# Four blocks of six chunks: a 20-product scheme over whole experts in a Mamba-2 and expert-merge kernel

## The chip, the cores and the metric

One core of a Trainium2 chip runs the whole kernel. The time is the device time of one execution in microseconds; it is taken several times, and the median is quoted. One execution was also taken by the hardware profiler, and all views below come from that one. PE is the matrix engine, PEld its weight loads, DVE the vector engine, ACT the scalar engine, POOL the general engine, and SP the engine whose queue issues nearly all transfers.

## What is computed

There are two stages. The first is a chunked state-space scan (4 sequences, 8 heads, 768 positions, head width 32, state width 16). The second merges four experts over the same 3072 tokens of width 256, with the tokens' heads laid side by side.

```python
# stage 1, per chunk: la = log(clip(a)); cum = cumsum(la)
M = (C @ B.T) * exp(cum_i - cum_j) * causal
y = M @ x + (C @ state) * exp(cum_i)
state = exp(sum la) * state + sum_j exp(cum_last - cum_j) * B_j x_j
# stage 2, x = y laid out as (3072, 256); E = 4, F = 1024
p = probs / (probs.sum(-1, keepdims=True) + 1e-9)
for e in range(E):
    out += p[:, e:e+1] * (maximum(x @ w1[e], 0) @ w2[e])
```

All of it is float32.

## The kernel before

The kernel works with 24 chunks of 128 positions. Two chunks make a *pair* of 256 tokens. The 16 *slices* of the hidden dimension are 256 wide, four to an expert. A *block product* is one 256-wide slice half against 256 tokens: `product()` issues it as two matmul calls (two 128-row halves of the contraction) into one bank of PSUM, and the profile shows four matmul records for it. Every matmul of the experts is issued there, so line L913 carries all of them.

Plain block multiplication of a slice with a pair takes two products a layer for each output half. The kernel saves products by bilinear schemes in the manner of Strassen: sums of weight blocks times sums of token blocks, and combinations of the results.

- Scheme `B` covers two slices x two halves x two pairs in 7 products for 8.
- Scheme `H` covers three slices x two halves x three pairs in 15 products for 18.

`ORDER` cuts the tokens into five blocks: three of four chunks (`B`) and two of six (`H`). Within a block a *unit* is one expert under `B` (two pairs of slices) or three slices under `H`; 16 slices do not divide by three, so that each `H` block has a sixth unit with one plain slice. For each unit and layer:

- `operands()` loads the weights, forms the sums of weight blocks (`scheme.sums`, line L1004) on DVE or POOL, and stores them in DRAM (`w_d`); later blocks load the stored sums. The sums for `H` are formed early, on POOL, at the units in `EARLY`.
- `token_sums()` forms the sums of token blocks, once a block (L1023).
- `twos_first()` and `threes_first()` issue the first layer's products. Results are kept with copies by ACT (`snap`, L922), put back into a bank to go on accumulating (`seed`, L927), corrected on DVE (`combine`, L940; a subtraction in the bank, L1050 or L1089), and then gated: `gated` (L948) does the ReLU and the multiplication by the expert's probability in one DVE instruction.
- `twos_right()` and `threes_right()` form the second layer's inputs from the gated blocks (`combine`, L940).
- `second()` issues the second layer by *houses*, pairs of accumulators that share a bank. `visit()` seeds the bank from the accumulator's copy, adds the products, and copies it back by ACT (L1190).
- `result()` combines a block's accumulators into its output (L1242); `leave()` transposes on DVE (L1287) and stores. The last block leaves by `leave_last()`, with transposes on PE (L1311).

The second layer of a unit is merged with the first layer of the next: `put()` spreads the two lists evenly in PE's order. PE's order is thus written out in `line`. Scans for the next block are put into it at positions in `PAIRS_AT`: `scores()` for the matmuls of C and B (L487), `outputs()` for the chunk's outputs and state (L531, L859). The decay matrix of chunks 0 to 3 is made by scans on DVE (L504); that of the later chunks by exponentials on ACT (L511) with a causal cut on POOL (L516), from cumulative sums that went through DRAM (`cum_d`).

The orders of the other engines come from `Plan.run()`, which places each step at build time by expected durations and due times, chooses between DVE and POOL where both can do it, and hands out buffers: 33 of kind V (gated blocks, copies, accumulators), 28 of kind W (weights), 8 banks. The engines' queues are fixed by that; at run time they only wait for each other.

Of the kernel before, what the change touches and what calls it, by code (L numbers as in the profile page):

```python
# [22 lines left out]
NV, NW = 33, 28  # L23
SLACK, BACK, YIELD = 0.0, 3.0, 0.0
EARLY = 2, 3, 4, 5, 6, 7, 8, 9, 10, 11
SOFT = 1
ROUND = 0, 3, 2, 0, 4
# [8 lines left out]
SCORED = 4  # L36
BUSY, CALM = 200.0, 1.06
AHEAD = 3
SOON = 3
BARE = 2  # L40
EASY = 40.0
HELD = ("x", "w"), (5, 8), (0, 7)
APART = (0, 7),
TAILS = 4, 4, 2, 0, 0, 0
LAST = (0, 1), (0, 2), (1, 1), (1, 2), (0, 0), (1, 0)
LATE = (13, 2), (6, 9), (11, 4), (10, 12), (3,), (1, 14), ("x", "w"), (5, 8), (0, 7)

PAIRS_AT = {
    (0, 2): ((1, 9, "s0"), (2, 1, "s1"), (2, 18, "o01")),
    (4, 2): ((0, 1, "s0"), (2, 1, "s1"), (2, 14, "o01")),  # L50
    (4, 3): ((0, 1, "s0"), (1, 1, "o0"), (1, 1, "s1"), (2, 1, "s2"), (2, 14, "o12")),
    (6, 3): ((0, 1, "s0"), (0, 14, "o0"), (2, 1, "s1"), (3, 1, "s2"), (3, 14, "o12")),
}
# [27 lines left out]
class Plan:  # L81
# [12 lines left out]
    def add(self, on, fn, reads=(), writes=(), part=(), lag=None, due=None, reuse=None, two=False,  # L94
            port=True, after=None, kb=0, hold=0.0, pieces=1, behind=()):
        w = Work(on, fn, (.16 if "PE" in on else .09) if lag is None else lag)
        w.hold = hold
        w.two, w.port, w.after, w.kb, w.pieces = two, port, after, kb, pieces
# [49 lines left out]
    def homed(self, w, at):  # L148

        taken, when = {}, at  # L150
        for v in w.touched:
# [7 lines left out]
            if v.seeded:  # L159
                spare = [h for h in spare if h.full]  # L160
            elif v.kind == "bank":
                hollow = [h for h in spare if not h.full and h.free <= at]
                spare = hollow or spare
# [24 lines left out]
    def run(self, line, at, begin):  # L188
# [19 lines left out]
        while todo:  # L208
# [4 lines left out]
            for w in waiting[e]:  # L213
# [5 lines left out]
                if len(w.on) > 1 and e == "POOL":  # L219
                    if max(ready, now) + w.on[e] > w.latest + late + SLACK or self.backlog(  # L220
                            waiting["DVE"], now, t["DVE"], w) < (BACK if now > EASY else 99):
                        continue
# [81 lines left out]
class Scheme:  # L304
# [4 lines left out]
H = Scheme()  # L309
H.rows, H.pairs = 3, 3  # L310
H.blocks = dict.fromkeys(
    (1, 2), {3: (0, 0), 9: (0, 1), "b": (1, 0), 13: (1, 1), 7: (2, 0), 0: (2, 1)})
H.sums = ((12, "b", 13, 1), (2, "b", 7, 1), (11, 12, 7, 1), (5, 11, 0, 1), (10, 3, 12, 1),
          (8, 10, 9, 1), (1, 8, 0, 1), (6, 1, 7, 1), (14, 5, 9, 1), (4, 3, "b", 1))
H.tokens = (("e", (0, 2), (0, 0), -1), (11, "e", (1, 2), -1), ("g", (1, 2), (1, 0), -1),
            (2, (1, 2), (0, 2), -1), (13, "g", "e", -1), (6, (0, 0), (0, 1), 1),
            (3, 6, (0, 2), -1), (10, "e", (1, 1), -1), (14, (1, 2), 6, -1),
            (4, (1, 1), (0, 1), -1), (1, 6, (1, 1), -1), (9, (1, 1), "g", -1))
H.right = {0: (1, 0), 5: (1, 2), 7: (0, 0), 8: (1, 1), 12: "e"}
H.shared = {1: ((12, 11), (6, 5), (2, 10), (14, 8), (4, 1)),  # L320
            2: ((2, 11), (4, 1), (14, 6), (5, 8), (10, 12))}
H.houses = ((13, 2), (11, 4), (0, 7), (1, 14), (6, 9), (5, 8), (10, 12), (3,), ("x", "w"))
H.plain = {(0, 0): 7, (1, 0): 0, (1, 1): 8, (1, 2): 5, (0, 1): "x", (0, 2): "w"}
# [7 lines left out]
B.right = {1: (0, 0), 2: (1, 0), 3: (1, 1)}  # L331
B.shared = {1: ((6, 7), (5, 3)), 2: ((7, 5), (6, 3))}
B.houses = ((1, 2), (3, 7), (5, 6), (4,))
ORDER = B, B, B, H, H
# [9 lines left out]
def kernel(  # L344
# [24 lines left out]
    NG = 5  # L369
# [4 lines left out]
    for scheme in ORDER:  # L374
        blocks.append(Block(scheme, sum(b.n for b in blocks)))
    assert NSEQ == 4 and E * EPB == 3 * NG + 1 and sum(b.n for b in blocks) == NCH

# [28 lines left out]
    def some(n, shape, name, pool=const):  # L406
# [15 lines left out]
        "gate": some(3, [P, max(b.n for b in blocks), P], "gate"),  # L422
# [23 lines left out]
    def load_decays(c, ab):  # L446
        src = acut_d if c < NSEQ else cum_d
        nc.sync.dma_start(
            out=ab, in_=src[real(c)].rearrange("h s -> (h s)").partition_broadcast(P))
# [120 lines left out]
    for fb in range(0, 4, 2):  # L570
        load_w1(fb, homes["W"][fb])
# [47 lines left out]
    for fb in range(4, 8, 2):  # L619
        load_w1(fb, homes["W"][fb])  # L620
    load_tokens(3, xb[3])
    for fb in range(0, 4, 2):
        load_w2(fb, homes["W"][fb + 1])
    load_decays(3, homes["ab"][0])
# [139 lines left out]
    def fetch(c):  # L764
# [9 lines left out]
        if "ab" not in s and c >= SPREAD:  # L774
            s["ab"] = value("ab")
            dma(lambda e: load_decays(c, s["ab"].t), 1, 512, part=[s["ab"]],
                reads=[cd] if c >= NSEQ else [])

    def decays(c):
# [5 lines left out]
        if c < NSEQ:  # L785
            for part in range(2):
# [4 lines left out]
                else:  # L791
                    half = NH * P // 2
                    dve(1.15, lambda e, lo=half * part: scan(
                        LT0[:, j], s["ab"].t[:, lo:lo + half], lo), two=True,
# [29 lines left out]
    def scores(cs):  # L824
# [6 lines left out]
        for r in (3, 2, 0, 1):  # L831
            def fn(e, r=r):
# [3 lines left out]
                nc.vector.tensor_mul(to, g, LT0[:, js, h] if cs[0] < NSEQ else to)  # L836

            dve(D512 if len(cs) > 1 else D256, fn, reads=[gs_[r], *(LTv if cs[0] < NSEQ else ())],
# [6 lines left out]
    def outputs(cs):  # L845
# [23 lines left out]
        for c in cs:  # L869
# [5 lines left out]
                out=yt.t[:, :, lo:lo + P], in_=v(y)[:, :, 0:P]), reads=[y], part=[yt])  # L875
            if c < NCH - NSEQ:
                s["A"] = value("A")
                act((.1, .4, .2, .4)[turn_of(c)], lambda e, c=c, s=s, y=y: keep_state(
                    c, s["A"].t, v(y)[:, :, P:]), reads=[y], part=[s["A"]])
# [89 lines left out]
    def operands(k, scheme, fbs, l, after=None, due=None, loaded={}):  # L969

        load, half = ((load_w1, w1_half), (load_w2, w2_half))[l - 1]
        where = {}
        for f, fb in enumerate(fbs):
            v = loaded.get((fb, l)) or value("W")
            used = {x[1] for r, x in scheme.blocks[l].items() if x[0] == f and r != "b"}
            if (fb, l) in loaded:
                pass
            elif len(used) == 1 and (*fbs, l, 0) in w_d:
                i, = used
                dma(lambda e, v=v, fb=fb, i=i: nc.sync.dma_start(  # L980
                    out=half(v.t, i), in_=source(fb, l, i).rearrange(
                        "p (j f) -> p j f", j=JJ) if l == 1 else source(fb, l, i)),
                    kb=128, part=[v], after=after)
            else:
                dma(lambda e, v=v, fb=fb: load(fb, v.t), part=[v], after=after)
            for r, x in scheme.blocks[l].items():
                if x[0] == f:
                    where[r] = v, x[1]
        shared = [value("W") for _ in scheme.shared[l]]
        for v, pair in zip(shared, scheme.shared[l]):  # L990
            for j, r in enumerate(pair):
                where[r] = v, j

        def view(r):
            v, i = where[r]
            return (half if r in scheme.blocks[l] else w1_half)(v.t, i)

        keys = [(*fbs, l, i) for i in range(len(shared))]
        if keys[0] in w_d:
            for key, v in zip(keys, shared):  # L1000
                dma(lambda e, v=v, key=key: nc.sync.dma_start(out=v.t, in_=w_d[key]), part=[v])
        else:
            for r, x, y, sign in scheme.sums:
                plan.add({"POOL": .72} if due else B256, lambda e, r=r, x=x, y=y, sign=sign: (  # L1004
                    on(e).tensor_add if sign > 0 else on(e).tensor_sub)(view(r), view(x), view(y)),
                    two=True, reads=[where[x][0], where[y][0]], part=[where[r][0]])
            for key, v in zip(keys, shared):
                d = stored_sums(key)
                dma(lambda e, v=v, d=d: nc.sync.dma_start(out=d, in_=v.t), reads=[v],
                    due=due or (lambda v=v: v.readers[-1]))  # L1010
        weights[k, fbs, l] = where, view

    def token_sums(k):
        Y, scheme = {}, blocks[k].scheme

        def get(x):
            return (yT[k, x[1]], lambda v, i=x[0]: v.t[:, i]) if isinstance(x, tuple) else (
# [8 lines left out]
        for r in {r for h in scheme.houses for r in h} - {"x", "w"}:  # L1026
            tokens[k, r] = get(scheme.right.get(r, r))
# [7 lines left out]
    def opener(k, fbs, seq):  # L1035
# [3 lines left out]
        def mul(r, into=None):  # L1039
# [490 lines left out]
```

## Time and profile before

| | us |
|---|---|
| median of 3 runs | 626.41 (626.35 to 628.62) |
| the profiled execution: its own time | 627.55 |
| the profiled execution: span from first to last instruction | 625.8 |
| busy PE, PEld, DVE, ACT, POOL | 616.6, 526.3, 487.0, 328.2, 167.8 |
| L913, the expert products: records | 1572 + 824 + 244 = 2640 |
| granted PE clock | 1.000 |
| bytes moved by DMA | 127.46 MB, 63.7% of 16 engines' time on the main queue |

A line of groups names the source line, the engine, the operation, output <- inputs, shapes and the count; then the busy time, the mean duration in ns of one, and the engine's idle time just before them with what ended it. A line of the chain of waits gives a start, a length and what the time went to. Records of PE overlap, so the time for one product is read from the chain and not from the groups.

### The profile page before, as it was taken

What the parts mean: (1) busy time and instruction counts of PE and PEld (TensorE: products, weight loads), DVE (VectorE), ACT (ScalarE), POOL (GpSimd) and SP (SyncE); (2) the same over time, 40 slices, a digit from 0 to 9 for tenths busy, and PEclk for the clock granted to TensorE, in tenths of its full rate; (3) what the DMA queues carried; (4) which work ended last, traced back from release to release, by engine and by line L of the source; (5) the groups of instructions that cost most, each with busy time, mean ns of one, the idle gap of its engine ahead of it and who ended that gap; (6) DMA issues with size and microseconds to landing.
All of it is one profiled execution on the core that took longest, in us unless ns stands there. A gap on an engine that the chain in (4) does not pass through costs nothing.

```text
span 625.8 us, 10435 instructions
## 1 busy us (share of the span) xinstructions
PE 616.6 (99%) x3429; PEld 526.3 (84%) x3429; DVE 487.0 (78%) x842; ACT 328.2 (52%) x763; POOL 167.8 (27%) x227
## 2 busy tenths in 40 slices
PE   9999989999999999999999999999999999999997
PEld 4788778888888888888888888888888888888886
DVE  6999998865638778475788997959897987869684
ACT  5477558634358644636855635446444335465441
POOL 4015645731135564424754102200000000000010
PEclk9999999999999999999999999999999999999999
DMA  7898879983799776579999828636232424953001
GB/s 235 275 346 272 279 244 316 321 285 98 218 306 305 234 241 210 146 235 339 305 358 317 267 48 260 204 103 193 62 93 67 130 44 111 351 161 114 1 1 50
DMA packets 112629, 127.46 MB, mean 204 GB/s; under 512 B 28980, under 2 KB 78144, under 8 KB 112576
## 3 DMA queue, kind: packets, MB, share of 16 engines
q1 hardware_dynamic: 112420, 126.74, 63.7%
q8 instruction: 27, 0.44, 0.3%
q14 instruction: 26, 0.21, 0.1%
q10 hardware_dynamic: 156, 0.06, 0.0%
HBM read 101.87 MB, written 24.89 MB: 203 GB/s over the span
## 4 chain that ended last, share of the span: by engine, by line
PE 91%; DVE 4%; DMA 2%; ACT 2%; issue 1%; SPq 0%; DVEq 0%; ACTq 0%
PE bank L913 86%; PE bank L487 2%; PE bank L531 2%; DMA ab<-cum_d 1%; DVE w L1004 1%; DVE v L940 1%; DVE v L948 1%; PE bank L669 1%; PE bank L859 1%; DMA w<-in_w_dram 0%; PE bank L645 0%; ACT MT L511 0%; DVE bank L1089 0%; ACT bank L927 0%; DVE MT L836 0%
## 5 line engine op out<-in xcount | busy, mean ns | idle before, releaser
L913 PE MATMUL bank<-v,w 128*128 128x256 f32 x1572 | 376.7, 380 | 3.2 <-DVE v L948 1.7
L913 PEld LDWEIGHTS bank<-v,w 128*128 128x128 f32 x1572 | 296.6, 190 | 49.2 <-issue 2.9
L913 PE MATMUL bank<-Y,w 128*128 128x256 f32 x824 | 210.6, 379 | 0.0
L913 PEld LDWEIGHTS bank<-Y,w 128*128 128x128 f32 x824 | 156.3, 190 | 21.9 <-issue 0.3
L940 DVE TENSOR_TENSOR v<-v,v 128x512 f32<-128x512 f32 x187 | 132.7, 730 | 33.6 <-ACT v L922 32.4
L948 DVE SCALAR_TENSOR_TENSOR v<-bank,gate 128x512 f32<-128x512 f32 x149 | 102.0, 687 | 45.7 <-PE bank L913 36.4
L927 ACT COPY bank<-v 128x512 f32<-128x512 f32 (+1 forms) x177 | 99.6, 571 | 58.1 <-DVE v L940 43.6
L922 ACT COPY v<-bank 128x512 f32<-128x512 f32 x101 | 58.9, 584 | 82.5 <-PE bank L913 80.6
L1004 POOL TENSOR_TENSOR w<-w,w 128x256 f32<-128x256 f32 x93 | 76.4, 840 | 54.8 <-PE bank L913 31.5
L1190 ACT COPY v<-bank 128x512 f32<-128x512 f32 x95 | 55.4, 584 | 65.8 <-PE bank L913 65.4
L913 PE MATMUL bank<-LT,w 128*128 128x256 f32 x244 | 62.6, 380 | 0.0
L511 ACT ACTIVATE MT<-ab,neg 128x128 f32<-128x128 f32 x160 | 51.2, 390 | 6.1 <-DMA ab<-cum_d 3.2
L913 PEld LDWEIGHTS bank<-LT,w 128*128 128x128 f32 x244 | 46.0, 190 | 7.1 <-issue 0.7
L516 POOL TENSOR_SCALAR_AFFINE_SELECT MT<-MT 128x512 f32<-128x512 f32 x40 | 29.8, 747 | 81.3 <-ACT MT L511 76.1
L940 DVE TENSOR_TENSOR v<-bank,v 128x512 f32<-128x512 f32 x37 | 25.4, 688 | 8.9 <-PE bank L913 6.9
L940 POOL TENSOR_TENSOR LT<-LT,v 128x512 f32<-128x512 f32 x1 | 1.6, 1580 | 110.5 <-DVE LT L940 110.5
L940 POOL TENSOR_TENSOR v<-v,v 128x512 f32<-128x512 f32 x4 | 6.2, 1546 | 75.7 <-DVE v L948 73.4
L836 DVE TENSOR_TENSOR MT<-bank,MT 128x512 f32<-128x512 f32 x40 | 24.8, 680 | 1.8 <-PE bank L487 1.6
L948 DVE SCALAR_TENSOR_TENSOR LT<-bank,gate 128x512 f32<-128x512 f32 x23 | 15.8, 686 | 11.3 <-PE bank L913 7.8
L940 DVE TENSOR_TENSOR v<-v,LT 128x512 f32<-128x512 f32 x29 | 22.3, 768 | 0.6 <-PE bank L913 0.2
L1004 DVE TENSOR_TENSOR w<-w,w 128x256 f32<-128x256 f32 x45 | 21.4, 507 | 0.3 <-DMA w<-in_w_dram 0.3
L1089 DVE TENSOR_TENSOR bank<-bank,v 128x512 f32<-128x512 f32 x22 | 15.3, 694 | 6.8 <-PE bank L913 6.7
(115 smaller groups left out, 372.2 us busy)
## 6 DMA issues: line engine op xcount, KB each, us to landing
w<-w_d SPq DMA_DIRECT2D x138, 256.0 KB
w<-in_w_dram SPq DMA_DIRECT2D x126, 256.0 KB
w_d<-w SPq DMA_DIRECT2D x82, 256.0 KB
ab<-cum_d SPq DMA_DIRECT2D x20, 512.0 KB
w<-in_w_dram SPq DMA_DIRECT2D x42, 128.0 KB
gate<-p_d SPq DMA_DIRECT2D x10, 384.0 KB
xb<-in_xbc_dram SPq DMA_DIRECT2D x17, 192.0 KB
gate<-p_d SPq DMA_DIRECT2D x11, 256.0 KB
```

The costliest lines, as they stand in the source:

```text
L487: nc.tensor.matmul(out=views[r][:, j], lhsT=xb[j][k, OBT:OBT + P], rhs=ctm[j][k].rearrange("p t s -> p (t s)"), start=(j == 0), stop=True, ...
L511: nc.scalar.activation(out=MT[:, place(c, h), 0:P], in_=ab[:, h * P:h * P + P], func=AF.Exp, bias=neg[:, h % NT, NQ * real(c) + h // NT:NQ ...
L516: nc.gpsimd.affine_select(out=MT[:, h:h + n, 0:P], in_=MT[:, h:h + n, 0:P], compare_op=ALU.is_ge, fill=0.0, base=0, pattern=[[0, n], [1, P ...
L836: nc.vector.tensor_mul(to, g, LT0[:, js, h] if cs[0] < NSEQ else to)
L913: nc.tensor.matmul(out=o, lhsT=w[:, j], rhs=x if half is None else x[:, j], start=(start and j == 0), stop=(j == 1), skip_group_check=True)
L922: act(.5, lambda e: nc.scalar.copy(out=flat(v), in_=bank.t), reads=[bank], writes=[v])
L927: act(.54 if to - lo > FB else .32, lambda e: nc.scalar.copy(out=bank.t[:, lo:to], in_=flat(v)[:, lo:to]), reads=[v], writes=[bank])
L940: plan.add(engines, lambda e: (on(e).tensor_add if sign > 0 else on(e).tensor_sub)(flat(v), whole(x), whole(y)), reads=[x, y], writes=[v], ...
L948: dve(D512, lambda e: nc.vector.scalar_tensor_tensor(out=h.t, in0=whole(x).rearrange("p (j m) -> p j m", j=JJ), scalar=0.0, in1=g.t[:, 2 * ...
L1004: plan.add({"POOL": .72} if due else B256, lambda e, r=r, x=x, y=y, sign=sign: (on(e).tensor_add if sign > 0 else on(e).tensor_sub)(view(r ...
L1089: dve(D512, lambda e: nc.vector.tensor_sub(b5.t, b5.t, flat(t)), reads=[t], writes=[b5])
L1190: act(.5, lambda e: nc.scalar.copy(out=flat(v), in_=bank.t), reads=[bank], writes=[v])
```

## The change

All tokens go in four blocks of six chunks under a new scheme `G`: four slices x two halves x three pairs, 20 products for 24. A unit is one expert. The schemes `H` and the plain sixth unit are gone. The first unit (expert 0, block 0) is different, because at that time only the first pairs of chunks exist: its first pair goes plain, the second and third by `B`, and `fold()` adds what `B` accumulated into the accumulators of `G`. The order of experts in each block is such that the last expert of a block is the first of the next, whose weights are then still there; so expert 0's sums for `G` are first formed at the end of the second block. `operands()` forms all sums the first time an expert is met (POOL where it can, DVE where a sum is late, by `lean`), stores them, and from then on loads them, with the four unsummed halves that the scheme needs packed in two buffers. `result()` works in the accumulators themselves. Chunks 4 and 5, which now belong to the first block, get their decays by scans on DVE. Buffers of kind V are 35, gates 2 instead of 3.

```diff
-NV, NW = 33, 28
+NV, NW = 35, 28
-EARLY = 2, 3, 4, 5, 6, 7, 8, 9, 10, 11
+LEAN = 4.0
+SCANNED = 6
+SCORED, OWN, LEAD, LEFT, MARK = 5, 3, 5, 3, 5
+FILLED = 3
+ORDERS = (0, 1, 2, 3), (3, 1, 2, 0), (0, 1, 2, 3), (3, 1, 2, 0)
+PAIRS_AT = ((1, 24, "s0"), (2, 1, "o0"), (2, 1, "s1"), (2, 24, "s2"), (3, 1, "o12")), (
+    (1, 1, "s0"), (1, 24, "s1"), (2, 1, "o01"), (2, 24, "s2"), (3, 1, "o2"))
...
             elif v.kind == "bank":
-                hollow = [h for h in spare if not h.full and h.free <= at]
+                hollow = [h for h in spare if not h.full and (
+                    h.free <= at or sum(x.full for x in spare) <= FILLED)]
...
-                if len(w.on) > 1 and e == "POOL":
+                if w.lean:
+                    if e == "DVE" and w.latest + late > max(ready, now) + LEAN:
+                        continue
+                elif len(w.on) > 1 and e == "POOL":
...
+G = Scheme()
+G.pairs = 3
+G.blocks = dict.fromkeys((1, 2), {
+    "a": (0, 0), 16: (0, 1), "c": (1, 0), 10: (1, 1), 13: (2, 0), "d": (2, 1), 11: (3, 0), "e": (3, 1)})
+G.raw = (16, 10), (13, 11)
+G.sums = ((15, 13, 10, -1), (9, 11, 10, -1), (0, "a", 16, -1), (2, "c", 11, -1), (1, "c", 13, -1),
...
+G.houses = (house(7, 9), house(15, 10), house((2, 19), (3, 17)), house(11, 13), house(12, 14),
+            house(4, 8), house((1, 6), (5, 18)), house(0, 16))
...
-ORDER = B, B, B, H, H
+BLOCKS = 4
...
-        if c < NSEQ:
+        if c < SCANNED:
             for part in range(2):
...
+    def fours_first(k, fbs):
...
+        b10 = mul(10)
+        s31 = snap(b10)
+        b13 = mul(13)
+        s23 = snap(b13)
+        adjust(b10, s23, -1)
+        b16 = mul(16)
+        s14 = snap(b16)
+        adjust(b13, s14)
+        b11 = mul(11)
+        s26 = snap(b11)
+        mul(15, b10)
+        s18 = snap(b10)
+        mul(9, b11)
+        b3 = adjust(b11, s31, 1, value("bank", seeded=True))
+        mul(0, b16)
+        gate(0, 0, b16)
+        mul(2, b11, [b3])
+        s20 = snap(b11)
+        gate(1, 2, combine(b11, s31))
+        mul(1, b10)
+        gate(1, 1, b10)
+        adjust(b10, s20)
+        mul(14, b13)
+        s19 = snap(b13)
+        gate(3, 2, mul(3, b3))
+        gate(1, 0, mul(7, b10))
+        gate(2, 1, mul(18, seed(s18)))
+        gate(2, 2, mul(17, b13))
+        adjust(b13, s23, -1)
+        b8 = mul(8, seed(s14))
+        b6 = adjust(b8, s26, -1, value("bank", seeded=True))
+        gate(0, 2, mul(19, seed(s19)))
+        mul(5, b8, [b6])
+        gate(3, 1, combine(b8, s26, -1))
+        gate(0, 1, mul(6, b6))
+        gate(2, 0, mul(12, b13))
+        gate(3, 0, mul(4, b8))
...
+    def fours_right(h):
+        T = {0: h[0, 0], 3: h[3, 2], 4: h[3, 0], 6: h[0, 1], 7: h[1, 0], 12: h[2, 0], 18: h[2, 1],
+             19: h[0, 2]}
...
+        T[11] = combine(T[9], v, -1, reuse=v)
+        T[13] = combine(w, T[15], -1)
...
+        into(9, A[9], A[10])
+        into(14, A[14], A[13])
...
+        if k < len(blocks) - 1:
+            for r, sign, x in parts.values():
+                into(r, A[r], A[x], sign)
+            return [A[r][0] for r in (0, 1, 2)]
...
+    plain = [plain_first(fb) for fb in range(4)]
...
+    own_ = visit(0, house(0, 16), [
+        (((0,), (16,))[d], weights["S", fb, 2], lambda fb=fb, d=d: w2_half(weights["S", fb, 2].t, d),
+         plain[fb][1]) for fb in range(4) for d in range(2)])
+    line.extend(own_[:OWN])
+    outputs([2, 3])
...
+    line.extend(fill[:SCORED - OWN])
+    scores([4, 5])
+    line.extend(fill[SCORED - OWN:len(fill) - LEFT])
+    outputs([4, 5])
...
+    for k in range(BLOCKS):
+        for g in ORDERS[k][not k:]:
+            units.append((k, tuple(range(4 * g, 4 * g + 4))))
```

## Prediction

> **What bounds the kernel now.** I read the page first, then the chain of waits, PE's waits, a table by stages, and the vector groups in two stretches.
>
> ```profile
> span 625.8 us, 10435 instructions
> ...
> PE 616.6 (99%) x3429; PEld 526.3 (84%) x3429; DVE 487.0 (78%) x842; ACT 328.2 (52%) x763; POOL 167.8 (27%) x227
> ...
> PE   9999989999999999999999999999999999999997
> ...
> DVE  6999998865638778475788997959897987869684
> ...
> L913 PE MATMUL bank<-v,w 128*128 128x256 f32 x1572 | 376.7, 380 | 3.2 <-DVE v L948 1.7
> ...
> L913 PE MATMUL bank<-Y,w 128*128 128x256 f32 x824 | 210.6, 379 | 0.0
> ...
> L913 PE MATMUL bank<-LT,w 128*128 128x256 f32 x244 | 62.6, 380 | 0.0
> ```
>
> PE is busy for 99%. The three groups of L913 (the expert products) hold 1572 + 824 + 244 = 2640 matmul records. Reading the loops gives the same work as block products: a block under B is 8 pairs of slices x 7 x 2 layers = 112, three of them 336; a block under H is 5 triples x 15 x 2 plus 12 plain = 162, two of them 324; 660 in all, so four records to a product. What one costs in the queue is read from long pieces of the chain of waits, since single records overlap:
>
> ```profile
> 241.48 0.59 PE bank L859 x16
> 242.07 1.12 PE bank L531 x32
> ...
> 281.13 0.72 PE bank L859 x32
> 281.86 2.10 PE bank L531 x64
> ...
> 335.48 39.91 PE bank L913 x184
> ...
> 417.61 199.63 PE bank L913 x924
> ```
>
> 39.91 / 46 = 0.868 us and 199.63 / 231 = 0.864 us: a product is 0.866 us. The upper lines are the chunk outputs: 1.71 us for a pair of chunks alone, 2.82 us for two pairs together. The rest of the span is small: some 13 us before the first product, about 4 us after the last, and these waits:
>
> ```profile
> PE bank L913 <- DVE v L948: 1.7, 1, 1.7
> PE bank L913 <- ACT bank L927: 1.3, 2, 0.7
> PE bank L487 <- ACT v L1193: 1.1, 1, 1.1
> ```
>
> The table by stages (busy us of PE, PEld, DVE, ACT, POOL in each window) puts them in time:
>
> ```profile
> 13.00:46.00 33.00, 32.60 (x191) 26.43 (x184) 30.07 (x63) 20.91 (x57) 2.33 (x4) 1.00 0.94 314
> 46.00:100.00 54.00, 50.63 (x335) 42.20 (x334) 50.53 (x85) 35.60 (x100) 28.12 (x40) 1.00 0.86 275
> ...
> 335.00:600.00 265.00, 265.00 (x1345) 231.61 (x1338) 217.87 (x364) 129.45 (x258) 17.73 (x15) 1.00 0.46 140
> ```
>
> PE idles 0.4 us up to 46 and 3.4 us from 46 to 100, where DVE is 94% busy; 0.6 us more near 199, then nothing to the tail: 4.4 us in flight. From 335 to 600, all H, DVE at 82% costs PE nothing. So the time is products times 0.866 us plus chunk work, and DVE is the next limit, first of all in the opening.
>
> **The change part by part.** *Products.* The new kernel has 16 (block, expert) units; 15 run scheme G, 20 products for each of two layers, so 600. The first (expert 0, block 0) runs before all three pairs exist: pair 0 plain, 4 slices x 2 x 2 layers = 16; pairs 1 and 2 by B, 2 x 7 x 2 = 28. Together 644, that is 16 fewer, all on PE's queue: 16 x 0.866 = -13.9 us. This is the main term.
>
> *Chunk matmuls.* The same 24 chunks. Grouping of outputs: before, two doubles in B (2 x 2.8), then twice a single and a double (9.0; the last is smaller), about 14.4 us; after, one single (1.7) and three times single plus double (13.3), about 15.0. Price +0.7 us.
>
> *Large vector work (128x512).* An H unit has 10 corrections, 9 gates, 13 second-layer sums: 32 for 30 products, 1.07 each. B has 20 for 28, 0.71. G has 8 corrections, 12 gates, 16 second-layer sums: 36 for 40, 0.90. Totals are 566 before and 564 after. G thus loads DVE less than the H stage, which hides its work completely: 36 x 0.69 = 24.8 us in a unit of 40 x 0.866 + about 1.7 chunk work = 36.3 us. On the path: 0. If that cover went, it would be paid as in the third rival.
>
> *Small vector work (128x256, 0.42 us).* Result sums: 7 per B block and 23 per H block = 67 before; 22 per block and 8 in fold() = 96 after. Token sums 36 before, 52 after. Together 45 x 0.42 = +19 us of DVE over the whole run, 3 points of its share, beside PE. Result sums have a unit to finish in; token sums of a new block read pairs that are put out a unit ahead. 0 on the path; late, each transition could cost the five-sum chain to G's first product, 2.1 us x 3. The in-place results leave 8 accumulators where an H block held 9 and 7 more buffers, so I see no new buffer wait there.
>
> *ACT.* A G unit has 7 snapshots, 3 seeds and up to 16 house copies, 26 x 0.58 = 15 us of 36: hidden. Chunks 4 and 5 move from 16 exponentials (16 x 0.39 = 6.2 us of ACT) and 4 causal cuts on POOL to 4 scans on DVE at the 1.22 us which the row of L504 for chunk 3 shows: +4.9 us of DVE before about 32 us.
>
> *Weights.* Sums: 164 before (104 on POOL at 0.84 us, 60 on DVE at 0.5), spread over two thirds of the run. After: 16 for the first unit and 32 for each expert, 144. Those of experts 1 to 3, 96 of them, fall due between about 46 and 186 us. POOL alone needs 32 x 0.84 = 27 us a unit, and about 5 us of chunk work, in 36 us: it fits with little to spare, and DVE takes what is late. SP's queue carries fewer weight bytes: 8 units reloaded at 40 x 131 KB (42 MB), 4 built at 2.1 MB in and 4.2 MB out (25 MB), 2 MB for the first; 69 MB, against 96 MB in the rows of loads and stores now. A reloaded unit moves 5.2 MB in 36 us, 145 GB/s; the H stage ran at 140 GB/s with no PE wait. A unit holds 20 of the 28 weight buffers, more than H's; loads that wait for a buffer hold up what is behind them on SP (gates, chunk inputs, result stores), but none stands late for PE in the H stage. 0, with the bound in the first rival.
>
> *Opening.* Two stretches pull apart. The own second-layer products put 7 products (6.0 us) between the first scores and their outputs, where 16 records (3.8 us) do it now: a gain of at most the 0.4 us lost there. Against it, expert sums, four more scans and twelve G token sums meet B's work on DVE; and the stored decays must come back for chunk 4 by about 33 us. Its row: the store leaves at 28.9 now and must leave near 20. Bounds on all PE stalls in flight: 0 (everything hidden, as after 200) and about 18 (twice the rate of 46 to 100, 2 x 3.4 / 54, held to 186). I take 6.0 us, nearest to the row of 46 to 100, for a stage of similar density that lasts about twice as long but has fewer stores: +1.6 us against the 4.4.
>
> *Sharing between DVE and POOL.* Two stretches of the same trace, with many POOL sums and with none:
>
> ```profile
> L1004 POOL TENSOR_TENSOR w<-w,w 128x256 f32<-128x256 f32 x19 | 16.7, 897 | 13.7 <-PE bank L913 7.8 <-DMA w_d<-w 5.7
> ...
> L940 DVE TENSOR_TENSOR v<-v,v 128x512 f32<-128x512 f32 x18 | 15.2, 868 | 3.5 <-ACT v L922 3.4
> ```
>
> ```profile
> L940 DVE TENSOR_TENSOR v<-v,v 128x512 f32<-128x512 f32 x18 | 11.8, 682 | 1.7 <-ACT v L922 1.7
> ```
>
> The first is 200 to 250, the second 450 to 500. An add of two buffers grows by 868 - 682 = 186 ns; 16 of them in a unit are 3 us, within the 11.5 us which a G unit leaves free on DVE. That is what I use. The Trainium skill, page "SBUF — State Buffer", section "Who interferes with whom", speaks against this change: the two engines share one port pair as an exclusive lock, held for the whole instruction, the loser fully blocked. If by that rule all 32 sums of a unit each held up DVE for their 0.72 us, it would be 23 us, 11.5 us over the slack, and three such units would make the sum 650 us. The rows agree with a lock that is sometimes met, not each time.
>
> *Tail.* Now: a plain unit's first six products, then 36 alone; after: 20 alone behind the last G first layer. Second-layer inputs of the last products (slice 3) are needed from the fourth house on, 6 products (5.2 us) later. 0, up to 2.
>
> *Sum* against the profiled execution's own 627.55 us (span 625.8): 627.55 - 13.9 + 0.7 + 1.6 = 615.95. The median of the runs shown lies 1.14 below that execution: 614.8, rounded to **615 us**.
>
> **The rivals.** (1) *Weight sums become the bound, slower than before.* While experts are first built, POOL sums slow to 1.18 us (three in 3.54 us at 220 in the timeline): 32 x 1.18 + 5 = 43 us against 36.3, and a first product waits for its weight: 6.5 us for each of experts 1, 2, 3, and perhaps 0: 19.5 to 26 us, giving 633 to 639. It decides from a unit losing 4.4 us (13.2 / 3). For: DVE is 94% busy in the opening and can't help. Against: DVE's own sum takes 0.42 us, and the sums run over 140 us, not just when needed. 0.13.
>
> (2) *The decays of chunks 4 and 5 come late.* One row in the chain, a load of stored decays, took 7.99 us under a saturated DMA. If outputs 4 and 5 wait that long, 3 to 8 us more than my sum: 618 to 623. For: DMA is at 0.94 there. Against: the new opening stores no weight sums ahead of it. 0.17.
>
> (3) *G's chain inside its banks.* One bank goes through six corrections, gates and seeds; each is ACT 0.58 + DVE 0.69, and 3.5 us of other products cover it. If DVE's backlog adds 0.5 to 1 us a unit, 15 units lose 7 to 15: 622 to 630, no measurable change. Against: H has such chains and PE shows no wait for them. 0.07.
>
> (4) *Stalls vanish.* Down to 1 us in flight: 609 to 611. 0.08.
>
> **How the numbers follow.** The forecast, 611 to 618, has the remaining 0.55. The range from 610 to 624 takes in it, the second rival, most of the fourth's upper part and the lower edge of the third: about 0.79. A difference of 0.5% (3.1 us) is about the least that a measurement of this kernel can tell. Faster: 0.55 + 0.17 + 0.08 = 0.80; same: 0.07; slower: 0.13.
>
> **What would show it.** Right: L913 with 2576 records (644 x 4) and 0.866 us a product in the chain; PE idle below 8 us between 13 us and the tail, most of it before 150; DVE near 82%; no recurring PE wait from 190 on. The first rival shows as PE waiting on w of L1004 or its loads at 75 and 114 us, the second as one PE wait at L859 or L531 near 33 us, the third as equal waits in every unit. More than 13 us of new PE idle makes the prediction wrong in sign.

## The result and the profile after

The changed kernel took 623.12 us (median of six executions, 621.46 to 624.35) beside 627.0 us of the kernel before on the same chip (six executions). The ratio is 0.9929, 95% interval 0.9903 to 0.9956: faster by 0.7%, some 4 us, where 11 to 12 us were forecast. The time is inside the range on record; the forecast of 615 us is missed by 8. The profiled execution took 624.35 us, 3.2 less than the profiled one of before.

The page of the changed kernel, the rows that answer to those of before (L924 is now the line of the products):

```profile
span 622.6 us, 10073 instructions
...
PE 606.6 (97%) x3365; PEld 515.1 (83%) x3365; DVE 498.7 (80%) x852; ACT 291.7 (47%) x681; POOL 180.9 (29%) x240
...
PE   9979989989999999999999999999999999999997
...
DVE  6879897998879987497877989487695988576675
...
POOL 6586962973262110696700110110000000000000
PEclk9999989999999999999999999999999999999999
...
L924 PE MATMUL bank<-v,w 128*128 128x256 f32 x1672 | 394.7, 381 | 5.2 <-DVE v L959 2.5
...
L924 PE MATMUL bank<-Y,w 128*128 128x256 f32 x692 | 177.7, 381 | 4.2 <-DVE bank L1062 1.8
...
L924 PE MATMUL bank<-LT,w 128*128 128x256 f32 x212 | 54.0, 380 | 0.0
```

1672 + 692 + 212 = 2576 records: 644 products, as forecast. PE's share fell from 99% to 97%. The digits say where: the slices (15.6 us each) that show a 7 or an 8 among PE's nines lie, but for the last, in the first ten, and one of them has a granted clock below nine. These ten hold more than half of POOL's work. The chain of waits gives the products when nothing is late:

```profile
280.56 69.26 PE bank L924 x320
...
427.16 185.83 PE bank L924 x860
```

69.26 / 80 = 0.866 us to a product, 185.83 / 215 = 0.864. So the unit price held, and what went wrong lies between products. PE's waits inside the span of the products, all before 156 us but that of the tail:

```profile
PE bank L924 <- DVE v L959: 2.5, 3, 1.8
PE bank L924 <- POOL w L1015: 2.0, 1, 2.0
PE bank L924 <- DVE bank L1062: 1.8, 1, 1.8
PE bank L924 <- DVE Y L1034: 1.4, 1, 1.4
PE bank L870 <- ACT v L1208: 0.9, 1, 0.9
...
PE bank L1316 <- DVE LT L1251: 0.7, 1, 0.7
PE bank L924 <- DMA w<-in_w_dram: 0.6, 1, 0.6
PE bank L924 <- ACT v L885: 0.4, 1, 0.4
PE bank L924 <- ACT bank L938: 0.4, 1, 0.4
```

They sum to 10.0 us without the tail's 0.7 (L1316); the forecast allowed 6.0, before had 4.4. One of them is for a weight sum on POOL (L1015, at 78 to 80 us), four are for DVE in the opening (34.7, 43.5, 51.7, 53.0 us), one is for DVE at 140 us. The table by windows right after the wait on POOL (busy us of PE, PEld, DVE, ACT, POOL; granted clock; DMA share; GB/s):

```profile
79.00:80.00 1.00, 0.02 (x1) 0.05 (x1) 1.00 (x3) 0.00 (x0) 1.00 (x3) 1.00 0.75 233
80.00:81.00 1.00, 1.00 (x3) 0.82 (x4) 1.00 (x3) 0.00 (x0) 1.00 (x2) 0.53 0.54 162
81.00:82.00 1.00, 1.00 (x4) 0.81 (x3) 0.63 (x3) 0.00 (x0) 1.00 (x3) 0.50 0.60 198
82.00:83.00 1.00, 1.00 (x3) 0.74 (x3) 0.68 (x1) 0.00 (x0) 1.00 (x3) 0.50 0.01 4
```

The wait is followed by over 3 us at half the clock, in which the first eight records take 3.66 us in place of 1.73: the wait costs 2.05 us and 1.9 behind it. A table by two long windows, the changed kernel first, the kernel before below:

```profile
13.00:155.00 142.00, 131.82 (x834) 107.55 (x828) 125.41 (x206) 76.79 (x215) 92.77 (x118) 0.99 0.66 214
155.00:612.00 457.00, 456.86 (x2422) 396.50 (x2421) 361.02 (x610) 208.35 (x450) 79.12 (x98) 1.00 0.47 145
```

```profile
13.00:155.00 142.00, 138.22 (x788) 116.25 (x781) 120.27 (x217) 85.97 (x222) 55.86 (x77) 1.00 0.84 275
155.00:612.00 457.00, 456.39 (x2513) 395.27 (x2512) 352.17 (x583) 235.14 (x523) 104.19 (x127) 1.00 0.59 186
```

After 155 us PE is as full as it was. Before, it loses 10.2 us where it lost 3.8; POOL works 92.8 us of the 142 where it worked 55.9, DVE is busy for 88% and gets through fewer instructions (206 for 217) in more time.

The balance by the starts of PE's records, after minus before: products 16 x 0.864 = -13.8 us; gaps between products +8.1 (15.0 for 6.9: above all the waits, 5.6 more, and the half clock, 1.9); all else, that is chunk work with its waits, the time ahead of the first product and the tail, +2.5 (51.7 for 49.2). Sum -3.2. The forecast had -13.9, +1.6 and +0.7.

### The profile page after: what moved, and what is told of

The parts are those of the page before. It is cut to its first block, busy times and chain, and to the rows that moved or that the text cites. A ratio compares the mean times of both kernels' runs of the same rounds, so it can differ in the third digit from the quotient of the medians.

```text
span 622.6 us, 10073 instructions
## 1 busy us (share of the span) xinstructions
PE 606.6 (97%) x3365; PEld 515.1 (83%) x3365; DVE 498.7 (80%) x852; ACT 291.7 (47%) x681; POOL 180.9 (29%) x240
## 4 chain that ended last, share of the span: by engine, by line
PE 82%; DVE 8%; DMA 5%; issue 2%; POOL 1%; ACT 1%; SPq 0%; DVEq 0%; POOLq 0%; ACTq 0%
PE bank L924 79%; DVE v L951 2%; DVE v L959 1%; DMA ah<-cum_d 1%; DMA ab<-acut_d 1%; POOL w L1015 1%; DMA w<-in_w_dram 1%; PE bank L498 1%; PE bank L542 1%; DVE Y L1034 1%; DMA acut_d<-v 1%; DVE w L1015 1%; DVE MT L847 1%; DMA ab<-cum_d 1%; PE bank L870 0%
## 5 line engine op out<-in xcount | busy, mean ns | idle before, releaser
L924 PE MATMUL bank<-v,w 128*128 128x256 f32 x1672 | 394.7, 381 | 5.2 <-DVE v L959 2.5
L924 PEld LDWEIGHTS bank<-v,w 128*128 128x128 f32 x1672 | 317.3, 191 | 53.0 <-issue 4.8
L924 PE MATMUL bank<-Y,w 128*128 128x256 f32 x692 | 177.7, 381 | 4.2 <-DVE bank L1062 1.8
L924 PEld LDWEIGHTS bank<-Y,w 128*128 128x128 f32 x692 | 130.0, 190 | 26.1 <-DVE bank L1062 2.4
L1015 POOL TENSOR_TENSOR w<-w,w 128x256 f32<-128x256 f32 x95 | 81.8, 882 | 34.4 <-PE bank L924 21.7
L1062 DVE TENSOR_TENSOR bank<-bank,v 128x512 f32<-128x512 f32 x86 | 58.6, 695 | 34.1 <-PE bank L924 23.2
L938 ACT COPY bank<-v 128x512 f32<-128x512 f32 x129 | 74.5, 591 | 12.3 <-DVE v L959 8.7
L924 PE MATMUL bank<-LT,w 128*128 128x256 f32 x212 | 54.0, 380 | 0.0
L924 PEld LDWEIGHTS bank<-LT,w 128*128 128x128 f32 x212 | 40.1, 190 | 6.0 <-DVE v L959 0.3
L1015 POOL TENSOR_TENSOR w<-w 128x256 f32<-128x256 f32 x32 | 27.0, 853 | 18.0 <-PE bank L924 12.3
L491 ACT ACTIVATE ctm<-xb,tmask 128x128 f32<-128x128 f32 x48 | 15.8, 391 | 10.3 <-DMA xb<-in_xbc_dram 10.0
L1251 DVE TENSOR_TENSOR v<-v,v 128x256 f32<-128x256 f32 x51 | 19.9, 425 | 0.8 <-ACT v L1204 0.5
L959 DVE SCALAR_TENSOR_TENSOR v<-v,gate 128x512 f32<-128x512 f32 x26 | 18.8, 724 | 0.4
```

Source lines behind the costliest of these rows:

```text
L924: nc.tensor.matmul(out=o, lhsT=w[:, j], rhs=x if half is None else x[:, j], start=(start and j == 0), stop=(j == 1), skip_group_check=True)
L938: act(.54 if to - lo > FB else .32, lambda e: nc.scalar.copy(out=bank.t[:, lo:to], in_=flat(v)[:, lo:to]), reads=[v], writes=[bank])
L959: dve(D512, lambda e: nc.vector.scalar_tensor_tensor(out=h.t, in0=whole(x).rearrange("p (j m) -> p j m", j=JJ), scalar=0.0, in1=g.t[:, 2 * ...
L1015: plan.add(B256, lambda e, r=r, x=x, y=y, sign=sign: (on(e).tensor_add if sign > 0 else on(e).tensor_sub)(view(r), view(x), view(y)), two= ...
L1062: dve(D512, lambda e: (nc.vector.tensor_add if sign > 0 else nc.vector.tensor_sub)(to.t, bank.t, whole(x)), reads=[x, bank], writes=[to])
L1251: plan.add(engines, lambda e: (on(e).tensor_add if sign > 0 else on(e).tensor_sub)(o[1](), x[1](), y[1]()), reads=[v for v in vs if v is n ...
```

## The experiments

Three theories of the gaps stood against each other. **A**: the sums of weights, now packed into the first 155 us (144 in all, formed when an expert is first met), load POOL and through it DVE. **B**: the stored decays of chunks 4 and 5 come back late; the load `ab<-acut_d` stands in the chain with 7.41 us from 24.18, and the wait at 34.7 hangs behind it. **C**: it is G's own chain between PE, ACT and DVE, as in the third rival. A was split later: **A1**, POOL has no time for the sums, as in the first rival; **A2**, POOL's reading of buffers slows DVE's sums, so DVE is late. All ratios are against runs of the kernel before on the same chip.

| kernel | median us | ratio, 95% interval |
|---|---|---|
| weight sums 8 columns wide | 616.57 | 0.9835, 0.9811 to 0.9859 |
| chunk 5's decays not loaded | 621.24 | 0.9920, 0.9894 to 0.9945 |
| both | 616.81 | 0.9841, 0.9816 to 0.9866 |
| POOL dearer in the plan | 621.66 | 0.9912, 0.9881 to 0.9944 |
| POOL fills, reads hardly | 616.65 | 0.9830, 0.9792 to 0.9869 |
| all weight sums on DVE | 628.90 | 1.0037, 1.0020 to 1.0055 |
| sums of three experts narrow | 618.26 | 0.9861, 0.9828 to 0.9893 |
| plan retuned | 620.83 | 0.9899, 0.9872 to 0.9926 |
| kernel before, POOL fills | 624.59 | 0.9974, 0.9964 to 0.9984 |
| plan retuned further | 618.17 | 0.9876, 0.9859 to 0.9894 |
| the change again, beside the last two | 622.65 | 0.9946, 0.9926 to 0.9966 |

**Sums made narrow.** In `operands()`, with the orders of all engines as they are (the edit in short):

```diff
-    on(e).tensor_add(view(r), view(x), view(y))
+    w = 8 if key in seen else P    # a buffer's first sum stays whole
+    on(e).tensor_add(view(r)[:, :, :w], view(x)[:, :, :w], view(y)[:, :, :w])
```

> The changed kernel with every queue in the same order, but 122 of its 144 weight sums are formed over 8 of each 128 columns only (the rest of those weights is left as it was in the buffer); transfers are unchanged. Theory A (the weight sums while experts are first built fill POOL and, through the data path they share, delay DVE): the PE waits at 80, 117 and 140 us go, with the slower clock after 80; the waits before 44 us stay in part; time 5 to 7 us lower, 616 to 618. Theory B (the opening's transfers): at most 1 us lower. Theory C (G's own chain between PE, ACT and DVE): less than 1 us lower, waits at 80 and 140 stay.

616.57 us. The gaps between products sum to 6.85 us, the figure of the kernel before, and PE's waits to 4.4 us and the tail's 0.7. What is left of them:

```profile
PE bank L870 <- ACT v L1219: 1.6, 1, 1.6
PE bank L924 <- DVE v L959: 0.9, 2, 0.5
...
PE bank L924 <- DVE Y L1045: 0.7, 1, 0.7
```

The waits on POOL and on DVE at 140 are gone, and the program is the same but for the sums. Theory A has the larger part: 6.5 us by the medians, 5.9 by the two ratios; theory C is out for that part. The run eases POOL, the weight sums on DVE and the sharing between the two all at once, so that it does not yet tell A1 from A2.

**Chunk 5's decays not loaded.** In `load_decays` and, behind the dots, in the scans (the edit in short):

```diff
+    w = 32 if c == 5 else NH * P
...
-    s["ab"].t[:, lo:lo + half]
+    ident.rearrange("p h s -> p (h s)") if c == 5 else s["ab"].t[:, lo:lo + half]
```

> The changed kernel with the same orders, but the broadcast load of chunk 5's decays (512 KB) is cut to 16 KB and its scans read a constant tile instead (chunk 5's own decays are left out). Theory B: the 7.4 us that this load takes is what the DVE queue, and the gates behind the scan, wait for; the PE waits at 34.7 and 37.6 us (1.8 and 0.9) go, the one at 43.5 shrinks; 2 to 4 us lower, 619 to 621. Theory A: 0 to 1.5 us, since the later waits come from the sums and take up what was won. Theory C: nothing.

621.24 us, just outside the 619 to 621 of theory B. The timeline of PE (start, length, records, in brackets the idle time before):

```profile
49.96 1.13 PE L925 MATMUL bank<-v,w 128*128 128x256 f32 x4 [1.65 <-DVE v L960]
...
78.16 2.83 PE L925 MATMUL bank<-v,w 128*128 128x256 f32 x12 [2.05 <-POOL w L1016]
...
136.87 1.13 PE L925 MATMUL bank<-Y,w 128*128 128x256 f32 x4 [1.78 <-DVE bank L1063]
```

The wait at 34.7 went, and one at 49.96 grew from 0.5 to 1.65: DVE is late there whatever came before. The two later waits stayed within 0.01 us. B is worth two microseconds at most, and the interval of the ratio overlaps with that of the change.

**Both edits.**

> Both edits of the two kernels before together (sums narrow, chunk 5's decay load cut). If A and B are all of the shortfall, this comes within 1.5 us of the predicted sum without extra stalls: 613 to 615, with under 3.5 us of PE idle in flight. If something else holds (theory C), it stays above 617.

616.81 us, no better than the narrow sums alone; the forecast of a further gain is missed. Beside the narrow sums the transfer brings nothing more; that its lateness is covered once DVE is eased is a reading, not shown.

**POOL dearer in the plan,** so that the planner gives DVE more of the sums: `B512` 1.3 to 1.5, `B256` .72 to .80.

> The changed kernel, complete, with one number of the build-time plan changed: a POOL sum is planned at 0.80 us (512 wide: 1.5) where it was 0.72 (1.3); the profile shows 0.88 in the mean. The orders are made anew from it, so DVE takes more of the sums in time. Theory A, in the form that the plan trusted POOL too much: the waits at 80 and 140 us shrink, 2 to 4 us lower. Theory A in the form that there is too little of both engines: no gain, the waits only move, within 1.5 us of the changed kernel. Theory B: within 1 us.

621.66 us with 619.27 to 623.18: no clear difference. The wait at 140 went, that on POOL stayed (1.90 at 81.3), and the opening's waits were 1.7 to 1.9 each. Lateness was moved about.

**POOL busy, but hardly reading.** The test between A1 and A2. POOL's sums become two fills of the same buffer and a sum over 4 of each 128 columns, with about the same time on POOL (the edit in short):

```diff
+    if e == "POOL":
+        for _ in range(2):
+            nc.gpsimd.memset(view(r), 0.0)
+        w = 4
```

> The changed kernel with every queue in the same order and DVE's own weight sums whole, but each of POOL's 127 weight sums is replaced by two fills of its target (0.32 us each by the row of fills) and a sum over 4 of each 128 columns: about as long on POOL as the 0.88 us of a sum now, and hardly reading a buffer. What the rest of those weights should be is left out. Theory A1 (POOL's time is what is short: sums come late): time unchanged within 1.5 us, 621.5 to 624.5, the PE wait for a weight sum at 80 us stays. Theory A2 (POOL's reads hold up DVE's sums of two buffers, and DVE holds up POOL): DVE's busy time up to 155 us falls by 6 to 9 us from 125, the waits at 80 and 140 shrink; 617 to 619.5, most of what narrow sums gave.

616.65 us, the same as with narrow sums. POOL's largest groups between 13 and 155 us, in the changed kernel and then here (count, busy us, mean ns):

```profile
L1015 POOL TENSOR_TENSOR w<-w,w 128x256 f32<-128x256 f32 x63 | 54.9, 893 | 16.8 <-issue 10.2 <-PE bank L924 4.1 <-DMA w<-in_w_dram 2.4
```

```profile
L1019 POOL MEMSET w<- 128x256 f32 x172 | 53.4, 310 | 15.1 <-PE bank L924 10.2
L1021 POOL TENSOR_TENSOR w<-w,w 128x8 f32<-128x8 f32 x64 | 18.3, 285 | 5.8 <-DMA w<-in_w_dram 0.8
```

2 x 310 + 285 = 905 ns for 893, and POOL's total in that window is 93.59 us for 92.77. So POOL is as busy and the loss is gone: A1 is wrong. DVE's groups in the same window, the changed kernel and then this one:

```profile
L951 DVE TENSOR_TENSOR v<-v,v 128x512 f32<-128x512 f32 x34 | 29.0, 872 | 0.1
L959 DVE SCALAR_TENSOR_TENSOR v<-bank,gate 128x512 f32<-128x512 f32 x33 | 22.2, 681 | 7.4 <-PE bank L924 7.4
```

```profile
L951 DVE TENSOR_TENSOR v<-v,v 128x512 f32<-128x512 f32 x36 | 24.6, 702 | 0.8 <-ACT v L933 0.7
L959 DVE SCALAR_TENSOR_TENSOR v<-bank,gate 128x512 f32<-128x512 f32 x35 | 23.9, 684 | 9.6 <-PE bank L924 9.3
```

The sum of two buffers falls from 872 to 702 ns; the operation that reads a bank and one buffer stands at 681 and 684, untouched by POOL. Taking all forms, the 48 operations 512 wide that read two buffers (sums, and five gates) had a mean of 863 ns and have 699, the token sums (L1034, 24 of them) 555 and have 427: 48 x 0.164 + 24 x 0.128 = 11 us of DVE's time in these 142 us. The Trainium skill, page "SBUF — State Buffer", section "Who interferes with whom", says just this: a DVE instruction with two SBUF inputs contends with a GpSimd instruction that reads SBUF, not with one that only writes it. The rows agree in both halves. DVE's busy time in the window falls by 6.8 us, from 125.4 to 118.6, with more instructions done. That the fills leave zeros in part of the weights is a difference that might touch the clock (1.000 in all four executions); the narrow sums, with other data, gave the same time.

**All weight sums on DVE.** The plan gets `{"DVE": D256}` for them in place of `B256`, so the orders are made anew.

> The changed kernel, complete, with all 144 weight sums on DVE, in orders made anew. A sum costs 0.34 us there, back to back, and nothing on POOL collides with it; DVE gets some 40 us more to do, of which about 32 before 190 us, where it is 88% busy. Theory A2 (collision is most of the loss): about even, 620 to 625, since the DVE time that collisions cost is given back. Theory A1 or plain lack of both engines: DVE becomes the bound of the opening and PE waits for gates; 626 to 634.

628.9 us, slower than the kernel before; the "620 to 625" of A2 is missed. DVE is busy for 135.0 of the 142 us from 13 to 155 and PE's waits come to 12.3 us:

```profile
165.01 1.10 PE L924 MATMUL bank<-v,w 128*128 128x256 f32 x4 [1.20 <-DVE w L1015]
169.54 2.07 PE L924 MATMUL bank<-Y,w 128*128 128x256 f32 x4 [3.42 <-DVE Y L1034]
```

But POOL's reads did not go away. The orders made anew gave POOL other sums of two buffers, 24 of them 512 wide in this window (none in the changed kernel), most of them in this row:

```profile
L951 POOL TENSOR_TENSOR v<-v,v 128x512 f32<-128x512 f32 x17 | 23.9, 1409 | 18.1 <-DVE v L959 9.4 <-DVE v L951 6.5 <-issue 1.8
```

POOL is busy for 63.7 us, and a weight sum on DVE took 0.55 us in the mean where 0.34 was expected. So the run doesn't test A2. It shows that DVE has no room for these sums, and falls into the 626 to 634 of a lack of both engines.

**Narrow sums for experts 2, 3 and 0 alone;** those of the first unit and of expert 1, due first, stay whole (`w = 8` only where `k != "S" and fbs[0] != 4`).

> As the kernel with narrow sums, but the sums of the first unit and of expert 1 (the first built under G) stay whole; only those of experts 2, 3 and 0 are narrow. If the loss is the opening's (everything due before 80 us): most of it stays, 620 to 622. If it is the rate over the whole first block (three experts built one after the other, each with 32 sums): most of it goes, 617 to 618.5, with the PE waits at 80, 117 and 140 us gone and those before 60 us unchanged.

618.26 us, 1.7 more than with all of them narrow: so much belongs to the first unit and expert 1, and nearly 5 of the 6.5 us come from the later three. The waits of the opening (1.43, 1.00, 1.32, 0.54; they were 1.79, 0.90, 1.38, 0.53) stayed much as they were; that at 140 is gone, the one near 78 is 1.33 and on DVE.

**The plan retuned.** POOL's costs raised (.82 and 1.55; the trace shows 0.88 for the first), chunk work in other places, `LEAN` 8, `KEEP` 5.

> The changed kernel, complete, planned with POOL sums at 0.82 us (512 wide: 1.55) and with other places for the chunk work: first scores of chunks 4 and 5 after 3 of the fill products where it was 5, their outputs with 2 products left where it was 3, the first pair of block 1 after 20 where it was 24, its last outputs one place earlier, DVE allowed 8 us of lead for a late sum where it was 4, and 5 spare buffers kept where it was 4. Theory A: the same work, but spread so that fewer sums are late; the waits at 80 and 140 us go, those before 60 us stay at 4 to 5 us; 616 to 619. Plain lack of both engines (order doesn't matter): 621 to 624.

620.83 us; the 616 to 619 expected is missed. Waits of 1.95 and 1.81 us in the opening and 1.63 and 1.09 near 110 took the place of the old ones.

**Control: the kernel before, with POOL's sums as fills.** The same edit as above, on the kernel before.

> Control: the kernel before, same orders, with its 104 weight sums on POOL replaced as in the run without POOL's reads (two fills and a sum over 4 of each 128 columns; the rest of those weights is left out). If collisions are what the change added: the kernel before has 4.4 us of PE idle in flight and meets them only in part, so it gains 0.5 to 2.5 us, 624 to 625.8, clearly less than the 6.5 us that the changed kernel gained. If the same edit gains 5 us or more here too, collisions are no difference between the two kernels, and the shortfall has another cause.

624.59 us: 1.6 us, where the changed kernel won 6.5. Its one wait for DVE (1.7 us at 90.8) is gone. So collisions cost time before too, but the same edit is worth four times as much in the changed kernel. That one has 84 weight sums on POOL between 13 and 155 us (63 and 21 by form), the kernel before 38 (33 and 5), in a stage in which DVE has little room (85% busy before, 88% after).

The control also sets the two kernels side by side with POOL's reads gone from both. The gaps between products are then 8.1 us against 4.9, where they were 15.0 against 6.9: of the 8.1 us by which the change made the gaps grow, 4.9 go with the collisions and 3.2 stay. The change is then worth 0.9830 / 0.9974 = 0.9856 (each against the kernel before on its own chip), some 9 us.

**Retuned further.** POOL at .88 and 1.65, the first pair earlier and its outputs later (`14`, `2`, `1`, `24`, `3` in `PAIRS_AT`), `FILLED` 1, `WAIT` .2, `KEEP` 4; the rest as in the retuned plan.

> The changed kernel, complete, planned with POOL sums at 0.88 us, the mean that the profile shows, and places for the chunk work searched under that: first pair of block 1 after 14 products of the unit where it was 24, its first outputs and last outputs one and two places later, at most one full bank kept back, and else as in the first retuned kernel. If collisions can be dodged by order: 616 to 619.5, PE idle in flight under 8 us. If not: 620 to 623.

618.17 us (617.04 to 619.67), and the change again, beside it on the same chip:

> The changed kernel as it is, on the same chip and between the same runs of the kernel before, to set the retuned ones against: 621.5 to 624.5. Its clock in the records shows whether the slower stretch after the 2 us wait at 80 us comes in each execution: by the first six runs it came in four (clock 0.996 or 0.997) and cost 1.5 to 2 us.

622.65 us (620.91 to 626.2). The retuned kernel beats the kernel before and the change, and its executions and the change's don't overlap. Its longest waits:

```profile
PE bank L924 <- DVE v L959: 2.7, 3, 1.4
PE bank L924 <- DVE Y L1034: 1.9, 1, 1.9
PE bank L924 <- ACT bank L938: 1.6, 1, 1.6
```

No wait for a weight sum is left. DVE has 36 of the window's sums where it had 16 and POOL works 79.6 us where it worked 92.8; the sum of two buffers (the large group) takes 760 ns where it took 872. Not all of the gain is dodged collisions: of the 6.2 us between the two profiled executions (624.35 and 618.17), 4.2 are in the gaps between products and 2.0 in chunk work, which has other places too.

## Why the prediction was right or wrong

**Products, right:** 2576 records, 0.864 us each, -13.8 for -13.9.

**Late stages, right:** from 155 to 612 us PE idles 0.1 us. The third rival's chain in the banks, the reloaded weights and 36 large operations a unit cost nothing there, and DVE's share, 80%, is near the 82 forecast.

**Stalls, wrong; this is the step that failed.** The text took 6.0 us, and under 8 as the sign of being right; waits in flight came to 10.0, and the half clock behind one of them to 1.9: gaps of +8.1 for +1.6. The larger part of the cause is in the part on sharing between DVE and POOL. The size there was near: 186 ns more for a sum of two buffers, 16 a unit, 3 us a unit, is 11.7 us for the 3.9 units of 36.3 us in these 142, and the trace gave 11. That the totals agree so well is in part luck, since 7.9 of the 11 are the large operations that the text priced and 3.1 the token sums, which it did not. The step from there to nothing on the path ("within the 11.5 us which a G unit leaves free on DVE") was wrong: the slack of 11.5 us was that of a G unit by itself, with its 36 large operations. The units in which the sums are formed are the first block's, which also hold chunk work, token sums, the fold and the result sums; DVE had no such slack there, and the same text had counted DVE as 94% busy from 46 to 100. With POOL as busy but hardly reading, PE's gaps fell from 15.0 to 8.1 and its waits in flight from 10.0 to 5.2, below the 6.0 allowed, so this is shown, not only argued. By the medians it is 623.1 - 616.6 = 6.5 us of the 8.3 between 614.8 and 623.1.

Some 1.6 us of this kind were in the kernel before already, by the control; what the change added is 4.9. The 3.2 us of growth that stay with the reads gone from both are twice the +1.6 forecast, and they lie in the opening: up to 52 us PE waits 3.8 us with the fills, 5.2 in the changed kernel and 0.3 in the kernel before. Their cause is open.

Of the 6.5 us some part goes with the clock. Among 14 executions of the changed kernel, six had a mean clock of 1.000 and took 621.9 us in the mean, eight had 0.995 to 0.997 and took 623.8. With 621.9 - 616.6 = 5.3 the collisions have their price without it, and the remaining 1.2 goes with the clock. The forecast had no term for it.

**Chunk work, the time ahead of the first product and the tail:** +2.5 us for +0.7 (the forecast's own 15.0 and 14.4 give 0.6). These are the other 1.8 us of the miss. The first product starts at 13.2 us and the last one starts 4.9 us before the end in both kernels, so the growth is in the chunk work and the waits between; not split further. The tail's wait is 0.7 us in every variant of the changed kernel, inside the "0, up to 2" on record.

**First rival** (weight sums as the bound): its sign in the profile appeared, PE waiting for L1015 at 78 us, near the 75 on record, but once, for 2.05 us, and its mechanism is not what was at work: POOL had the time. It was priced by how much POOL is slowed; the loss came through what POOL does to DVE.

**Second rival** (late decays): the wait exists and the load took 7.41 us, near the 7.99 it was priced by, but removing it won two microseconds at most and nothing once DVE was eased. The time fell into the band it named, 618 to 623, at its edge, by another cause.

**The rule weighed against the trace.** The full price by the lock, 650 us, was far too high, but zero was the wrong end. What the Trainium skill says on the page "SBUF — State Buffer", section "Who interferes with whom", that such instructions collide, holds here. The mean hides how. Of the 34 sums in the group of 872 ns, 20 took 0.67 to 0.69 us and ten 1.20 to 1.23 (the row gives the shortest, the middle and the longest, in ns):

```profile
L951 DVE TENSOR_TENSOR v<-v,v x34: 674/680/1231, 48.8 to 152.4; 128x512 f32<-128x512 f32 x34
```

So most sums are untouched, and many of the others are held up by half a microsecond; the price of 650 us had every one held up for 0.72. The row of 868 beside 682 already showed the mean. What was missing was the question of when the collisions fall.

**Open:** waits of 0.4 to 2 us before 52 us stand in every variant of the changed kernel, for DVE, ACT and POOL by turns; they sum to 3 to 5 us. Which queue must be eased there was not settled; easing one moved the wait to the next.

## What to carry to other kernels

When work is moved to a free engine, ask what it reads at the same time as its neighbour, and charge the neighbour's slowdown to the stage in which the work falls, by that stage's own busy shares, not by those of a clean unit. To tell "too slow" from "in the way", keep the engine busy for the same time with something that reads nothing, and run the same edit on the kernel before as a control. A plan whose costs come from an engine running alone is worth retuning: with dearer POOL sums and other places for the chunk work the same change won 8 us in place of 4. Dearer sums alone (0.80) gave no clear gain, so that how much of it the costs bring is not shown.

## What the runs showed of the hardware

Fills on POOL hardly slow DVE, sums do, and in these rows only where DVE reads two buffers: 872 ns beside sums and 702 beside fills for two buffers (682 in the stretch of the kernel before without POOL sums), 681 and 684 for a bank and a buffer.

A wait of 2.05 us on PE was enough for the granted clock to fall to 0.50 for over 3 us, but not each time: another execution of the same kernel shows the same wait (2.0 us for L1015, up to 79.28) and a clock of 1.00 in every window from 76 to 84, two of which are:

```profile
80.00:81.00 1.00, 1.00 (x6) 0.89 (x5) 1.00 (x3) 0.00 (x0) 1.00 (x2) 1.00 0.67 217
82.00:83.00 1.00, 1.00 (x6) 0.90 (x5) 1.00 (x3) 0.00 (x0) 1.00 (x3) 1.00 0.07 16
```

With all sums on DVE, waits of 1.20 and 3.42 us close together (163.8 to 169.5) came with a clock of 0.61 from 168 to 172 and 0.53 from 172 to 176:

```profile
168.00:172.00 4.00, 2.46 (x6) 1.68 (x7) 4.00 (x9) 0.35 (x1) 1.20 (x2) 0.61 0.54 199
172.00:176.00 4.00, 4.00 (x11) 3.22 (x10) 1.78 (x6) 1.90 (x4) 0.00 (x0) 0.53 0.76 258
```

The Trainium skill, page "TensorE: Matmul & The Clock Gate", section "Part 1: The HAM clock gate (the “warmup” mystery)", has the clock fall after an idle window of some 3.4 us, with windows that run freely. The 2.05 us here are below that length, and PE was full up to the wait's start at 77.93 (1.93 us busy from 76 to 79). The measurement decides: a wait of this length can cost nearly as much again.
